# Attention and gated MLP layer on one core: the ordering list in blocks of four matmuls, a GpSimd product, head sums of two slices, three residual buffers, and the spatial weights' load behind the last transpose

## The chip, the cores and the metric

The kernel runs on one core of a Trainium2 chip. A core has a matrix engine (TensorE, PE in the profile, with its weight loads as PEld), a vector engine (VectorE, DVE), a scalar engine for activations and casts (ScalarE, ACT), a general engine (GpSimd, POOL) and an engine that mostly issues DMAs (SyncE, SP). Each works through its own queue in order; semaphores join them. PSUM holds what matmuls accumulate, SBUF all other data on the chip. The metric is the device time of one execution in microseconds (us).

## The reference

2048 rows of 1024 values in bfloat16, one layer of two halves: local attention with 32 heads of 32 values, where each row sees itself and seven earlier rows at steps of two, then a gated MLP whose gate mixes all rows.

```python
def _A_ref(x, wqkv, wo):                  # H = 32, Dh = 32, W, dil = 8, 2
    q, k, v = split(x @ wqkv)
    idx = pos[:, None] - off[None, :]     # off = 0, 2, ..., 14
    logits = einsum('bhsd,bhswd->bhsw', q, k[idx]) * Dh ** -0.5   # masked where idx < 0
    attn = softmax(logits)
    return einsum('bhsw,bhswd->bhsd', attn, v[idx]) @ wo
def _B_ref(x, w_in, w_sp, b_sp, w_out):   # F = 3584, Fh = 1792
    z = gelu(x @ w_in)
    z1 = z[..., :Fh]
    z2 = layernorm(z[..., Fh:])
    g = einsum('ts,bsf->btf', w_sp, z2) + b_sp
    return (z1 * g) @ w_out
h = x + _A_ref(layernorm(x), A_wqkv, A_wo)
h2 = h + _B_ref(layernorm(h), B_w_in, B_w_sp, B_b_sp, B_w_out)
```

## The kernel before

The rows are cut into four chunks of 512 (index `c`), each of four blocks of 128 rows (`il`). Up to line 751 the chunks go through these steps; after it comes a last phase that mixes all rows.

- `ln1(c)`: the first layernorm of the chunk, with a transpose through memory.
- `qkv(c)`: the three projections on PE, 24 groups of 8 matmuls (line 351). Two groups share one accumulator. ScalarE casts it out (lines 358 and 363).
- `attention(c)`: the work of DVE. For each of the eight window places a product of q and the shifted k, 4096 values a partition (line 407), which is then folded by adding halves: 4096 to 2048 values (`add1`, line 411) and, in mode 2, 2048 to 1024 (`add2`, line 414). PE sums the folded slices over the head's lanes with small matmuls (line 430) into `L`. `LMODE` gives each chunk its mode, the number of slices that are left for PE. In mode 2 one sum takes four window places and 8 matmuls of 512 columns, and a chunk has two sums; in mode 4 it takes two places and 16 matmuls of 256 columns, and a chunk has four. Then come the maximum (line 439), the exponential on ScalarE (line 449), the sum and its reciprocal, the broadcast of the weights by PE (line 483) and its copies (line 488), and eight products with the shifted v, added up (lines 501, 504, 510).
- `head(c)`: the output projection on PE, 64 matmuls (line 554), then on DVE the residual sum (line 563) with x from a small buffer `xr` (`XRB` buffers, loaded at line 558), on ScalarE the squares (line 568), the moments in `batch_rstd`, and the normalised rows, transposed by a DMA on SyncE's queue into `hnT` (line 601; line 586 for chunk 3, block by block).
- `b_z2(c)` and `b_z1(c)`: the two halves of the first MLP product on PE (lines 627 and 677), with gelu on ScalarE. z1 goes to memory; z2 is squared (line 643), normalised (lines 656 and 658) and stored.
- `batch_rstd`: four small operations on DVE (lines 519 to 522), a power of -1/2 on GpSimd (line 524), and, where it serves four blocks at once, one small product on DVE again (line 529): minus mean times the root, named nb, which ScalarE's normalisation uses as its bias.
- `wsp0`, line 743: loads the first quarter of the spatial weights by a transposing DMA on SyncE's queue (line 695).
- The last phase, lines 763 to 803: for each chunk 224 matmuls with the spatial weights (line 773), the gate on DVE (lines 776 and 777) and the output projection (line 788).

The order within PE, ScalarE, DVE and GpSimd up to line 751 is not the order of the program. Every step is put on a list with `add(engine, cost in us, function, what it needs, prio, lat, take, free)`, and `Order.run` plays the list through with these costs: it takes the engine on which something can start first, among its steps that can start then (within 0.02 us) the one with the lowest `prio`, and notes its place. `take` and `free` count the three accumulators and other buffers. A need is met `lat` (0.1 us, unless told otherwise) after the needed step's end. The instructions are then written down in that order, and on the chip each engine keeps to it, whatever the real times are. PE's large groups have `prio` 6 and up in the order of the program; head projections have 4 and up, the small sums and broadcasts 1. `LSLACK` and `BSLACK` (2 us) hold a head sum or a broadcast back in the list after its last input. DMAs (`dma_op`) are on the list too, with a place but no engine.

A group of 8 matmuls on PE is one step of 1.727 us in `qkv` and `b_z1`; in `head` and `b_z2` half a block (8 matmuls) is one step. The second step of an accumulator needs the first, 0.1 us after its end.

Of the kernel before, what the change touches and what calls it, by code (L numbers as in the profile page):

```python
# [10 lines left out]
FP32 = mybir.dt.float32  # L11
BF16 = mybir.dt.bfloat16
ALU = mybir.AluOpType
# [7 lines left out]
P = 128  # L21
NT = S // P
CH = 512
NCH = S // CH
# [8 lines left out]
NWARM = 14  # L33
XRB = 2
LMODE = (2, 2, 4, 4)
LSLACK, BSLACK = 2.0, 2.0
Z2ACT = (4, 4, 4, 0)
LNPRIO = (0, 2.0, 2.5, 4.0)
LAST_COLS = ((0, 512), (512, 768), (768, 1024))
# [85 lines left out]
def kernel(  # L125
# [35 lines left out]
    eps_t = cpool.tile([P, 1], FP32, name="eps_t")  # L161
    V.memset(eps_t[:], EPS)
    nhalf = cpool.tile([P, TPC], FP32, name="nhalf")
    V.memset(nhalf[:], -0.5)
# [164 lines left out]
    def qkv(c):  # L329
        for xi in range(3):  # L330
            wv = wsb[xi][:].rearrange("p kt (m dl) -> p kt dl m", dl=DLO)
            for dp in range(DLO // 2):
                key = ("acc", "qkv", c, xi, dp)
                deps = [G.get(("xnT", c))]
                if c == 0 and xi == 0 and dp < 2:
                    def mm(wv=wv, dp=dp):
                        if dp == 0:
                            accs = [new_acc(), new_acc()]
                            G["acc", "qkv", 0, 0, 0], G["acc", "qkv", 0, 0, 1] = accs
                            for kt in range(KT):  # L340
                                for dl in range(4):
                                    T.matmul(accs[dl // 2][:, dl % 2, :], wv[:, kt, dl, :], xnT[0][:, kt, :],  # L342
                                             start=(kt == 0), stop=(kt == KT - 1))
                    last = add("PE", 6.91 if dp == 0 else 0.0, mm, deps, prio=order(), take="acc")
                else:
                    for j in range(2):
                        def mm(j=j, dl=2 * dp + j, wv=wv, key=key):
                            if j == 0:
                                G[key] = new_acc()
                            for kt in range(KT):  # L350
                                T.matmul(G[key][:, j, :], wv[:, kt, dl, :], xnT[c][:, kt, :],  # L351
                                         start=(kt == 0), stop=(kt == KT - 1))
                        last = add("PE", 1.727, mm, deps, prio=order(), take="acc" if j == 0 else None)
                        deps = [last]
                def ev(xi=xi, dp=dp, key=key):
                    if c == 0:
                        off = 0 if xi == 0 else HALO
                        A.copy(att_in[0][xi][:, 2 * dp:2 * dp + 2, off:off + CH], G[key][:])  # L358
                        if xi > 0 and dp == 3:
                            dma(qkv_d[xi][:, :, CH - HALO:CH], att_in[0][xi][:, :, CH:CH + HALO])  # L360
                    else:
                        stg = l1.tile([P, 2, CH], BF16, name="stg", tag="xn", bufs=4)
                        A.copy(stg[:], G[key][:])  # L363
                        dma(qkv_d[xi][:, 2 * dp:2 * dp + 2, c * CH:(c + 1) * CH], stg[:])
# [9 lines left out]
    def attention(c):  # L374
# [67 lines left out]
        prev = add("DVE", 1.18, mx, lms, prio=3.0, take="prod")  # L442
        exps = []
        for hw in range(2):
            ws = slice(4 * hw, 4 * hw + 4)
# [69 lines left out]
    def batch_rstd(key, sums, sqs, n, pfx, deps, prio, cols=TPC):  # L515
        def a1():
            t = {k: bp.tile([P, cols], FP32, name=pfx + k, tag=pfx + k) for k in ("mean", "msq", "var", "rstd", "nb")}
            G[key] = t
            V.tensor_scalar(t["mean"][:], sums(), 1.0 / n, None, op0=ALU.mult)
            V.tensor_tensor(t["msq"][:], t["mean"][:], t["mean"][:], op=ALU.mult)  # L520
            V.scalar_tensor_tensor(t["var"][:], sqs(), 1.0 / n, t["msq"][:], op0=ALU.mult, op1=ALU.subtract)
            V.tensor_scalar(t["var"][:], t["var"][:], 0.0, EPS, op0=ALU.max, op1=ALU.add)
        s1 = add("DVE", 0.74, a1, deps, prio=prio)
        s2 = add("POOL", 1.05, lambda: nc.gpsimd.tensor_tensor(G[key]["rstd"][:], G[key]["var"][:], nhalf[:, 0:cols], op=ALU.pow), [s1], lat=0.4)  # L524
        if cols < TPC:
            return s2
        def a3():
            t = G[key]
            V.scalar_tensor_tensor(t["nb"][:], t["mean"][:], -1.0, t["rstd"][:], op0=ALU.mult, op1=ALU.mult)
        return add("DVE", 0.16, a3, [s2], prio=prio)  # L530

    def head(c):
# [6 lines left out]
        for il in range(TPC):  # L539
            i = c * TPC + il  # L540
            deps = [G["avdone", c]]
            for half in range(2):
                def mm(half=half, il=il, i=i):
                    if half == 0:
                        if il == 0:
# [5 lines left out]
                        st["acc", il] = new_acc()  # L551
                    for dl in range(4 * half, 4 * half + 4):
                        for nh in range(2):
                            T.matmul(st["acc", il][:, nh, :], oTs[c][:, dl, il * P:(il + 1) * P], wo_sb[:, dl, nh * CH:(nh + 1) * CH],  # L554
                                     start=(dl == 0), stop=(dl == DLO - 1))
                def xr_load(k):
                    st["xr", k] = bp.tile([P, D], BF16, name="xr", tag="xr", bufs=XRB)
                    dma(st["xr", k][:], x2d[(c * TPC + k) * P:(c * TPC + k + 1) * P, :])
                m_ = add("PE", 1.727, mm, deps, prio=prio + il * 1e-2 + half * 1e-3, take="acc" if half == 0 else None)
                deps = [m_]  # L560
            def res(il=il, i=i):
# [11 lines left out]
        if last:  # L573
            G["close"] = dma_op(0.0, close_, [G["headmm", c]] + [G["z2n", k, il] for k in range(c) for il in range(TPC)])
            for il in range(TPC):
                rs = batch_rstd(("l2", c, il), lambda il=il: st["hsum"][:, il:il + 1], lambda il=il: st["hsq"][:, il:il + 1],
                                D, f"l2_{il}", [sqd[il]], 0.5, cols=1)
                def nrm(il=il):
                    t = G["l2", c, il]
                    V.tensor_scalar(st["hnc"][:, il, :], st["hnc"][:, il, :], t["mean"][:], t["rstd"][:],  # L580
                                    op0=ALU.subtract, op1=ALU.mult)
                n_ = add("DVE", 0.5, nrm, [rs], prio=0.6)
# [25 lines left out]
    def b_z2(c):  # L608
        st = {}
        sqd = []  # L610
        for il in range(TPC):
            evs = []
            for hf in range(2):
                wd = win_specs[hf][1]
                deps = [G.get(("hnT", c, il), G["hnT", c]), G["win", hf]]
                for half in range(2):
                    def mm(half=half, hf=hf, il=il, wd=wd):
                        if half == 0:
                            st["acc"] = G["accz", c, il, hf] = new_acc()
# [3 lines left out]
                        accf = G["accz", c, il, hf][:].rearrange("p a b -> p (a b)")  # L623
                        for kt in range(4 * half, 4 * half + 4):
                            for n0 in range(0, wd, CH):
                                n1 = min(n0 + CH, wd)
                                T.matmul(accf[:, n0:n1], hnTs[c][:, il, kt, :], wins[hf][:, kt, n0:n1],  # L627
                                         start=(kt == 0), stop=(kt == KT - 1))
                    m_ = add("PE", 1.727 if hf == 0 else 1.3, mm, deps, prio=order(), take="acc" if half == 0 else None)
                    deps = [m_]  # L630
                def ev(hf=hf, il=il, wd=wd):
# [18 lines left out]
        for il in range(TPC):  # L650
            i = c * TPC + il
            def nrm(il=il, i=i):
# [4 lines left out]
                else:  # L657
                    V.tensor_scalar(z2[:], st["u", il][:], t["mean"][:, il:il + 1], t["rstd"][:, il:il + 1], op0=ALU.subtract, op1=ALU.mult)
                if c < NCH - 1:
# [7 lines left out]
    def b_z1(c):  # L667
        for fp in range(NF // 2):
            deps = [G["hnT", c], G["win", 2 if fp < 4 else 3]]
            for j in range(2):  # L670
                def mm(j=j, fp=fp):
                    f = 2 * fp + j
                    wt, f0 = (wins[2], f) if f < 8 else (wins[3], f - 8)
                    if j == 0:
                        G["accy", c, fp] = new_acc()
                    for kt in range(KT):
                        T.matmul(G["accy", c, fp][:, j, :].rearrange("p (a b) -> p a b", a=TPC), wt[:, kt, f0 * P:(f0 + 1) * P],  # L677
                                 hnTs[c][:, :, kt, :], start=(kt == 0), stop=(kt == KT - 1))
# [155 lines left out]
```

## Time and profile before

| what | us |
|---|---|
| time, median of 3 runs | 737.73 (737.09 to 739.45) |
| the profiled execution, its own time | 737.65 |
| its span, first to last instruction | 735.9 |
| head sums, line 430: 32 matmuls of 512 columns, 128 of 256 | busy 2.5 and 5.0 |
| line 414, second fold, 16 of 683 ns | busy 10.4 |
| line 411, first fold, 32 of 1.22 us | busy 38.2 |
| line 407, window products, 32 of 2.28 us | busy 72.0 |
| line 524, power on GpSimd, 7 of four columns | busy 15.7 |
| line 529, small product on DVE, 7 of 0.16 us | busy 1.2, idle before it 5.8 |

The profiled execution is one run under the hardware profiler. Its span stands for what the queues show; 1.75 us of its time lie outside. Rows of the profile name a line, an engine, an operation, the tiles written and read (`acc<-xnT,wv`), the shape and a count; a row's bracket gives the idle time of that engine just before it and what ended it. The granted clock of PE was 0.998 of full speed over the span.

### The profile page before, as it was taken

Reading aid. Unit: us, or ns where it says so; the run is one execution under the profiler, and the core shown is the slowest. Engines: PE = TensorE matmul, PEld = TensorE weight load, DVE = VectorE, ACT = ScalarE, POOL = GpSimd, SP = SyncE. Lnnn points to the kernel's source line nnn. Section 1 sums busy time; section 2 is a strip of 40 time slices with the busy share of each in tenths; the row PEclk is TensorE's granted clock in tenths of the full one; section 3 lists DMA queues with packets and bytes.
Section 4 is the critical chain, followed back from the end, with each engine's and each line's share of the span. In section 5 each row is a group of like instructions: output and inputs, shape, how many; then the busy total and the mean of one; then the engine's idle time right before and its main releaser. Section 6 shows DMA issues by size and latency. Waiting matters only on the chain.

```text
span 735.9 us, 8608 instructions
## 1 busy us (share of the span) xinstructions
PE 725.7 (99%) x3580; PEld 369.1 (50%) x3580; DVE 416.8 (57%) x431; ACT 219.2 (30%) x267; POOL 50.0 (7%) x59
## 2 busy tenths in 40 slices
PE   7999999999999999999999999999999999999998
PEld 4666665566645444444444544444444444444444
DVE  4899899988999899889940012221232223212322
ACT  4322532534338954696563620000000000000000
POOL 0310200100102100300113000000000000000000
PEclk9999999999999999999999999999999999999999
DMA  9874563485484632370079988135104410020002
GB/s 337 315 242 116 191 184 122 153 231 200 149 324 109 210 113 74 115 227 18 29 229 338 256 243 268 40 95 148 58 29 112 133 57 31 28 86 29 1 15 71
DMA packets 113223, 105.27 MB, mean 143 GB/s; under 512 B 67776, under 2 KB 91744, under 8 KB 113056
## 3 DMA queue, kind: packets, MB, share of 16 engines
q1 hardware_dynamic: 105472, 72.63, 33.0%
q0 software_dynamic: 7280, 31.50, 12.1%
q8 instruction: 28, 0.46, 0.3%
q10 hardware_dynamic: 432, 0.59, 0.2%
q14 instruction: 11, 0.09, 0.0%
HBM read 55.09 MB, written 33.88 MB: 121 GB/s over the span
## 4 chain that ended last, share of the span: by engine, by line
PE 89%; DVE 7%; ACT 1%; POOL 1%; issue 1%; DMA 0%; POOLq 0%; DVEq 0%; ACTq 0%
PE acc L773 26%; PE acc L351 22%; PE acc L788 13%; PE acc L627 10%; PE acc L677 9%; PE acc L554 8%; DVE prod L504 2%; DVE oT L510 2%; PE acc L342 1%; DVE part L411 1%; POOL l3rstd L524 1%; PE L L430 1%; DMA xp<-in_A_x_dram 0%; PE tpa L252 0%; ACT z1s L683 0%
## 5 line engine op out<-in xcount | busy, mean ns | idle before, releaser
L773 PE MATMUL acc<-wspT,z2sb 128*128 128x512 bf16 x896 | 194.0, 379 | 0.0
L773 PEld LDWEIGHTS <-z2sb 128*128 128x128 bf16 x896 | 87.7, 98 | 105.7
L776 DVE TENSOR_TENSOR g<-acc,bB 128x1024 bf16<-128x1024 f32 x28 | 34.3, 1224 | 157.6 <-PE acc L773 133.0
L677 PE MATMUL acc<-hnT,win 128*128 128x512 bf16 x448 | 99.4, 379 | 0.5 <-ACT z1s L683 0.5
L627 PE MATMUL acc<-win,hnT 128*128 128x512 bf16 (+1 forms) x512 | 99.3, 352 | 0.0
L627 PEld LDWEIGHTS <-hnT 128*128 128x128 bf16 x512 | 49.8, 98 | 47.7 <-issue 0.9
L407 DVE TENSOR_TENSOR prod<-qT,kT 128x4096 bf16<-128x4096 bf16 x32 | 72.0, 2284 | 1.6 <-ACT kT L358 1.6
L788 PEld LDWEIGHTS <-zg 128*128 128x128 bf16 x462 | 45.2, 98 | 51.7
L677 PEld LDWEIGHTS <-win 128*128 128x128 bf16 x448 | 43.4, 98 | 52.5 <-issue 1.7
L504 DVE TENSOR_TENSOR prod<-vT,AB 128x4096 bf16<-128x4096 bf16 x28 | 63.8, 2289 | 1.0
L510 DVE TENSOR_TENSOR oT<-oT,prod 128x4096 bf16<-128x4096 bf16 x28 | 64.0, 2284 | 0.1
L363 ACT CAST stg<-acc 128x1024 bf16<-128x1024 f32 x36 | 36.4, 1011 | 78.6 <-PE acc L351 75.5
L788 PE MATMUL acc<-wout_a,zg 128*128 128x512 bf16 (+1 forms) x264 | 58.2, 373 | 0.0
L795 DVE TENSOR_TENSOR ot<-acc,hr 128x1024 bf16<-128x1024 f32 x15 | 18.4, 1224 | 69.4 <-PE acc L788 69.4
L351 PE MATMUL acc<-xnT,wv 128*128 128x512 bf16 x256 | 57.1, 380 | 0.0
L351 PE MATMUL acc<-xnT,wk 128*128 128x512 bf16 x256 | 57.1, 380 | 0.0
L554 PE MATMUL acc<-wo_sb,oT 128*128 128x512 bf16 x256 | 56.3, 379 | 0.7 <-DVE oT L510 0.7
L351 PE MATMUL acc<-xnT,wq 128*128 128x512 bf16 x224 | 49.8, 379 | 0.0
L351 PEld LDWEIGHTS <-wk 128*128 128x128 bf16 x256 | 36.4, 143 | 19.1 <-issue 0.9
L351 PEld LDWEIGHTS <-wv 128*128 128x128 bf16 x256 | 36.4, 143 | 19.1 <-issue 0.9
L788 PE MATMUL acc<-wout_b,zg 128*128 128x512 bf16 (+1 forms) x198 | 44.4, 373 | 0.0
L351 PEld LDWEIGHTS <-wq 128*128 128x128 bf16 x224 | 31.9, 143 | 16.8 <-issue 0.8
(125 smaller groups left out, 489.9 us busy)
## 6 DMA issues: line engine op xcount, KB each, us to landing
qkv_d<-stg SPq DMA_DIRECT2D x36, 256.0 KB, 2.5
z_d<-z1s SPq DMA_DIRECT2D x28, 256.0 KB, 2.6
z1c<-z_d SPq DMA_DIRECT2D x28, 256.0 KB, 2.7
z_d<-u SPq DMA_DIRECT2D x12, 448.0 KB, 2.9
z2sb<-z_d POOLq DMA_DIRECT2D x12, 448.0 KB, 9.2
xr<-in_A_x_dram SPq DMA_DIRECT2D x16, 256.0 KB, 2.8
h_d<-hb SPq DMA_DIRECT2D x16, 256.0 KB, 2.4
win<-in_B_w_in_dram POOLq DMA_DIRECT2D x2, 2048.0 KB, 9.1
```

Of the source, the lines that this page charges most:

```text
L351: T.matmul(G[key][:, j, :], wv[:, kt, dl, :], xnT[c][:, kt, :], start=(kt == 0), stop=(kt == KT - 1))
L363: A.copy(stg[:], G[key][:])
L407: V.tensor_tensor(st["prod"][:], qT[:], kT[:, :, o:o + CH], op=ALU.mult)
L504: V.tensor_tensor(pvs[w][:], vT[:, :, o:o + CH], abb, op=ALU.mult)
L510: prev = add("DVE", 2.3, lambda w=w: V.tensor_tensor(oTs[c][:], oTs[c][:], pvs[w][:], op=ALU.add), [prev, m_], prio=3.0, lat=0.15, free="p ...
L554: T.matmul(st["acc", il][:, nh, :], oTs[c][:, dl, il * P:(il + 1) * P], wo_sb[:, dl, nh * CH:(nh + 1) * CH], start=(dl == 0), stop=(dl == ...
L627: T.matmul(accf[:, n0:n1], hnTs[c][:, il, kt, :], wins[hf][:, kt, n0:n1], start=(kt == 0), stop=(kt == KT - 1))
L677: T.matmul(G["accy", c, fp][:, j, :].rearrange("p (a b) -> p a b", a=TPC), wt[:, kt, f0 * P:(f0 + 1) * P], hnTs[c][:, :, kt, :], start=(kt ...
L773: T.matmul(acc[:, j, :], z2sb[a][:, f * P:(f + 1) * P], wspT[:, a, :], start=(a == 0), stop=(a == NT - 1))
L776: V.tensor_tensor(g1[:], acc[:], bB[:, c * CH:(c + 1) * CH].unsqueeze(1).to_broadcast([P, 2, CH]), op=ALU.add)
L788: T.matmul(outs, zg[:, f, il * P:(il + 1) * P], wt[:, f0, lo:hi], start=(f == 0), stop=(f == NF - 1))
L795: V.tensor_tensor(ot[:], acc[:].rearrange("p a b -> p (a b)"), hr[:], op=ALU.add)
```

## The change

The edits:

1. `LMODE` is 2 for all four chunks.
2. PE's groups go on the list in blocks of four matmuls: in `qkv` and `b_z1` a group of eight is two steps of 0.863 us (`PIECES`), in `head` a block of rows has four steps instead of two, in `b_z2` too (0.863 or 0.653 us). The next block of an accumulator may follow at once (0.0 in place of the 0.1 us).
3. In `batch_rstd` the product nb moves from DVE to GpSimd, right behind the power; the list counts both as one step of 1.6 us whose result is there 1.2 us later. For this the mean is kept with a minus sign, and what subtracted it adds it.
4. In chunks 0 and 1 an exponential of one value per partition stands on ScalarE ahead of the real ones, as soon as the head sums are done.
5. `XRB` is 3: three residual blocks are loaded at the start of a head, and the fourth after the first block's squares.
6. `wsp0` needs chunk 3's last transpose too.
7. Names: `moments` and `root` for what was `a1`, the power and `a3`.

```diff
-XRB = 2
-LMODE = (2, 2, 4, 4)
+XRB = 3
+LMODE = (2, 2, 2, 2)
+PIECES = ((0, 0), (0, 4), (1, 0), (1, 4))
...
+    texp = cpool.tile([P, 1], FP32, name="texp")
...
-                    for j in range(2):
-                        def mm(j=j, dl=2 * dp + j, wv=wv, key=key):
-                            if j == 0:
+                    for j, k0 in PIECES:
+                        def mm(j=j, k0=k0, dl=2 * dp + j, wv=wv, key=key):
+                            if j == 0 and k0 == 0:
                                 G[key] = new_acc()
-                            for kt in range(KT):
+                            for kt in range(k0, k0 + 4):
                                 T.matmul(G[key][:, j, :], wv[:, kt, dl, :], xnT[c][:, kt, :],
                                          start=(kt == 0), stop=(kt == KT - 1))
-                        last = add("PE", 1.727, mm, deps, prio=order(), take="acc" if j == 0 else None)
-                        deps = [last]
+                        last = add("PE", 0.863, mm, deps, prio=order(), take="acc" if j == 0 and k0 == 0 else None)
+                        deps = [(last, 0.0)]
...
+        if c < 2:
+            add("ACT", 0.2, lambda: A.activation(texp[:], eps_t[:], ACTF.Exp), lms, prio=0.0, table="exp")
...
-            V.tensor_scalar(t["mean"][:], sums(), 1.0 / n, None, op0=ALU.mult)
-            V.tensor_tensor(t["msq"][:], t["mean"][:], t["mean"][:], op=ALU.mult)
+            V.tensor_scalar(t["nmean"][:], sums(), -1.0 / n, None, op0=ALU.mult)
+            V.tensor_tensor(t["msq"][:], t["nmean"][:], t["nmean"][:], op=ALU.mult)
...
-        s2 = add("POOL", 1.05, lambda: nc.gpsimd.tensor_tensor(G[key]["rstd"][:], G[key]["var"][:], nhalf[:, 0:cols], op=ALU.pow), [s1], lat=0.4)
-        if cols < TPC:
-            return s2
-        def a3():
-            t = G[key]
-            V.scalar_tensor_tensor(t["nb"][:], t["mean"][:], -1.0, t["rstd"][:], op0=ALU.mult, op1=ALU.mult)
-        return add("DVE", 0.16, a3, [s2], prio=prio)
+        def root():
+            t = G[key]
+            nc.gpsimd.tensor_tensor(t["rstd"][:], t["var"][:], nhalf[:, 0:cols], op=ALU.pow)
+            if cols == TPC:
+                nc.gpsimd.tensor_tensor(t["nb"][:], t["nmean"][:], t["rstd"][:], op=ALU.mult)
+        return add("POOL", 1.05 if cols < TPC else 1.6, root, [s1], lat=0.4 if cols < TPC else 1.2)
...
-            for half in range(2):
+            for part in range(4):
...
-                    for dl in range(4 * half, 4 * half + 4):
+                    for dl in range(2 * part, 2 * part + 2):
...
-                m_ = add("PE", 1.727, mm, deps, prio=prio + il * 1e-2 + half * 1e-3, take="acc" if half == 0 else None)
-                deps = [m_]
+                m_ = add("PE", 0.863, mm, deps, prio=prio + il * 1e-2 + part * 1e-3, take="acc" if part == 0 else None)
+                deps = [(m_, 0.0)]
...
-                        for kt in range(4 * half, 4 * half + 4):
+                        for kt in range(2 * part, 2 * part + 2):
...
-                    m_ = add("PE", 1.727 if hf == 0 else 1.3, mm, deps, prio=order(), take="acc" if half == 0 else None)
-                    deps = [m_]
+                    m_ = add("PE", 0.863 if hf == 0 else 0.653, mm, deps, prio=order(), take="acc" if part == 0 else None)
+                    deps = [(m_, 0.0)]
...
-            for j in range(2):
-                def mm(j=j, fp=fp):
+            for j, k0 in PIECES:
+                def mm(j=j, k0=k0, fp=fp):
...
-                m_ = add("PE", 1.727, mm, deps, prio=order(), take="acc" if j == 0 else None)
-                deps = [m_]
+                m_ = add("PE", 0.863, mm, deps, prio=order(), take="acc" if j == 0 and k0 == 0 else None)
+                deps = [(m_, 0.0)]
...
-    dma_op(0.0, wsp0, [G["z1ev", NCH - 2], G["close"]])
+    dma_op(0.0, wsp0, [G["z1ev", NCH - 2], G["close"], G["hnT", NCH - 1]])
```

The normalisations at lines 580 and 658 use `nmean` with an addition in place of `mean` with a subtraction.

More of the change, by code (lines that the diff above doesn't have):

```diff
@@ L515, in batch_rstd, with moments @@
     def batch_rstd(key, sums, sqs, n, pfx, deps, prio, cols=TPC):
-        def a1():
-            t = {k: bp.tile([P, cols], FP32, name=pfx + k, tag=pfx + k) for k in ("mean", "msq", "var", "rstd", "nb")}
+        def moments():
+            t = {k: bp.tile([P, cols], FP32, name=pfx + k, tag=pfx + k) for k in ("nmean", "msq", "var", "rstd", "nb")}
             G[key] = t
-            V.tensor_scalar(t["mean"][:], sums(), 1.0 / n, None, op0=ALU.mult)
-            V.tensor_tensor(t["msq"][:], t["mean"][:], t["mean"][:], op=ALU.mult)
+            V.tensor_scalar(t["nmean"][:], sums(), -1.0 / n, None, op0=ALU.mult)
+            V.tensor_tensor(t["msq"][:], t["nmean"][:], t["nmean"][:], op=ALU.mult)
             V.scalar_tensor_tensor(t["var"][:], sqs(), 1.0 / n, t["msq"][:], op0=ALU.mult, op1=ALU.subtract)
             V.tensor_scalar(t["var"][:], t["var"][:], 0.0, EPS, op0=ALU.max, op1=ALU.add)
-        s1 = add("DVE", 0.74, a1, deps, prio=prio)
-        s2 = add("POOL", 1.05, lambda: nc.gpsimd.tensor_tensor(G[key]["rstd"][:], G[key]["var"][:], nhalf[:, 0:cols], op=ALU.pow), [s1], lat=0.4)
-        if cols < TPC:
-            return s2
-        def a3():
+        s1 = add("DVE", 0.74, moments, deps, prio=prio)
+        def root():
             t = G[key]
-            V.scalar_tensor_tensor(t["nb"][:], t["mean"][:], -1.0, t["rstd"][:], op0=ALU.mult, op1=ALU.mult)
-        return add("DVE", 0.16, a3, [s2], prio=prio)
+            nc.gpsimd.tensor_tensor(t["rstd"][:], t["var"][:], nhalf[:, 0:cols], op=ALU.pow)
+            if cols == TPC:
+                nc.gpsimd.tensor_tensor(t["nb"][:], t["nmean"][:], t["rstd"][:], op=ALU.mult)
+        return add("POOL", 1.05 if cols < TPC else 1.6, root, [s1], lat=0.4 if cols < TPC else 1.2)
     def head(c):
@@ L541, in head, with mm @@
             deps = [G["avdone", c]]
-            for half in range(2):
-                def mm(half=half, il=il, i=i):
-                    if half == 0:
+            for part in range(4):
+                def mm(part=part, il=il, i=i):
+                    if part == 0:
                         if il == 0:
@@ L579, in nrm @@
                     t = G["l2", c, il]
-                    V.tensor_scalar(st["hnc"][:, il, :], st["hnc"][:, il, :], t["mean"][:], t["rstd"][:],
-                                    op0=ALU.subtract, op1=ALU.mult)
+                    V.tensor_scalar(st["hnc"][:, il, :], st["hnc"][:, il, :], t["nmean"][:], t["rstd"][:],
+                                    op0=ALU.add, op1=ALU.mult)
                 n_ = add("DVE", 0.5, nrm, [rs], prio=0.6)
@@ L615, in b_z2, with mm @@
                 deps = [G.get(("hnT", c, il), G["hnT", c]), G["win", hf]]
-                for half in range(2):
-                    def mm(half=half, hf=hf, il=il, wd=wd):
-                        if half == 0:
+                for part in range(4):
+                    def mm(part=part, hf=hf, il=il, wd=wd):
+                        if part == 0:
                             st["acc"] = G["accz", c, il, hf] = new_acc()
@@ L657, in nrm @@
                 else:
-                    V.tensor_scalar(z2[:], st["u", il][:], t["mean"][:, il:il + 1], t["rstd"][:, il:il + 1], op0=ALU.subtract, op1=ALU.mult)
+                    V.tensor_scalar(z2[:], st["u", il][:], t["nmean"][:, il:il + 1], t["rstd"][:, il:il + 1], op0=ALU.add, op1=ALU.mult)
                 if c < NCH - 1:
@@ L669, in b_z1 @@
             deps = [G["hnT", c], G["win", 2 if fp < 4 else 3]]
-            for j in range(2):
-                def mm(j=j, fp=fp):
+            for j, k0 in PIECES:
+                def mm(j=j, k0=k0, fp=fp):
                     f = 2 * fp + j
                     wt, f0 = (wins[2], f) if f < 8 else (wins[3], f - 8)
-                    if j == 0:
+                    if j == 0 and k0 == 0:
                         G["accy", c, fp] = new_acc()
-                    for kt in range(KT):
+                    for kt in range(k0, k0 + 4):
                         T.matmul(G["accy", c, fp][:, j, :].rearrange("p (a b) -> p a b", a=TPC), wt[:, kt, f0 * P:(f0 + 1) * P],
                                  hnTs[c][:, :, kt, :], start=(kt == 0), stop=(kt == KT - 1))
-                m_ = add("PE", 1.727, mm, deps, prio=order(), take="acc" if j == 0 else None)
-                deps = [m_]
+                m_ = add("PE", 0.863, mm, deps, prio=order(), take="acc" if j == 0 and k0 == 0 else None)
+                deps = [(m_, 0.0)]
             def ev(fp=fp):
```

## The prediction

> **What bounds the kernel now.** I read the page first: the busy shares, then the chain that ended last. TensorE (PE) holds 89% of that chain and is busy for 99% of the span; the vector engine (DVE) holds 7%, nearly all of it between 300 and 368 us.
>
> ```profile
> PE 725.7 (99%) x3580; PEld 369.1 (50%) x3580; DVE 416.8 (57%) x431; ACT 219.2 (30%) x267; POOL 50.0 (7%) x59
> ...
> PE 89%; DVE 7%; ACT 1%; POOL 1%; issue 1%; DMA 0%; POOLq 0%; DVEq 0%; ACTq 0%
> ```
>
> The 57% of DVE is a mean over two stages. By the timeline of DVE alone, from 42.23 us to 368.07 us it runs the four chunks' attention with hardly a pause, and PE fills in projections around it. After 368 us PE runs without any wait to the end. So the question is what PE loses before 368 us; the timeline of PE has it:
>
> ```profile
> 249.60 1.89 PE L677 MATMUL acc<-hnT,win 128*128 128x512 bf16 x8 [0.45 <-ACT z1s L683]
> ...
> 320.86 0.62 PE L430 MATMUL L<-part,csb 128*32 128x256 bf16 x16 [1.31 <-DVE part L411]
> ...
> 356.87 10.52 PE L677 MATMUL acc<-hnT,win 128*128 128x512 bf16 x48
> 368.13 13.99 PE L554 MATMUL acc<-wo_sb,oT 128*128 128x512 bf16 x64 [0.74 <-DVE oT L510]
> 381.95 10.52 PE L677 MATMUL acc<-hnT,win 128*128 128x512 bf16 x48
> 392.31 1.89 PE L627 MATMUL acc<-win,hnT 128*128 128x512 bf16 x8
> 394.04 1.89 PE L677 MATMUL acc<-hnT,win 128*128 128x512 bf16 x8
> ```
>
> Start, length, what, and in brackets the idle time before it. Three waits, 0.45 + 1.31 + 0.74 = 2.50 us in all. And a cushion: when the last head begins at 368.13, PE still has 48 + 8 = 56 matmuls of chunk 2's z1 in hand, which need nothing of chunk 3. At 1.727 us for 8 (the pitch 392.31 to 394.04) that is 12.1 us.
>
> **PE work that goes.** The chain shows a head sum of either kind at the same price:
>
> ```profile
> 74.65 0.55 PE L L430 x8
> ...
> 217.68 0.55 PE L L430 x16
> ```
>
> Chunks 2 and 3 do four sums each of 16 matmuls now and two each of 8 afterwards: 8 - 4 = 4 fewer, 4 x 0.55 = 2.2 us. The block of eight behind one takes 1.83 instead of 1.73 us, so up to 2.6; I take **-2.4 us**. Blocks of four instead of eight issue the same matmuls: 0. With every wait of the three gone too, the floor is 735.9 - 2.4 - 2.5 = 731.0 us.
>
> **What DVE gets in exchange.** Each of the 16 window products of chunks 2 and 3 gains the second fold of line 414. Its price stands in chunk 0:
>
> ```profile
> 46.64 2.35 DVE L411 TENSOR_TENSOR prod<-prod 128x2048 bf16<-128x2048 bf16 x2
> 48.91 1.28 DVE L414 TENSOR_TENSOR part<-prod 128x1024 bf16<-128x1024 bf16 x2
> 50.11 4.49 DVE L407 TENSOR_TENSOR prod<-qT,kT 128x4096 bf16<-128x4096 bf16 x2
> ...
> 307.51 0.16 DVE L529 SCALAR_TENSOR_TENSOR l2nb<-l2mean,l2rstd 128x4 f32<-128x4 f32 x1 [0.93 <-POOL l2rstd L524]
> ```
>
> Two folds from 48.91 to 50.11: 0.60 each, 16 x 0.60 = **+9.6 us**, all in the stage where DVE has no pause.
>
> The last line is what comes back. The small product nb leaves DVE, which now stands still for the root that GpSimd (POOL) computes. There are six such places before 368 us with waits of 0.93, 0.92, 0, 0.93, 0.90 and 0.90, sum 4.58, and 0.08 of pitch each, 0.5: at best -5.1 us. But why does that root take so long?
>
> ```profile
> 242.39 1.02 POOL L524 TENSOR_TENSOR l3rstd<-l3var,nhalf 128x4 f32<-128x4 f32 x1 [2.35 <-DVE l3var L522]
> ...
> 304.57 2.90 POOL L524 TENSOR_TENSOR l2rstd<-l2var,nhalf 128x4 f32<-128x4 f32 x1 [23.39 <-DVE l2var L522]
> ```
>
> 1.02 us beside a product that reads PSUM, 2.90 us beside a 4096-wide product with both inputs in SBUF (304.30 to 306.58); it ended 0.89 us after that product did. Now DVE won't pause behind it, and a second POOL operation follows. If DVE must stand aside for both, it pays 2 x 0.9 in each of six places, 10.8, instead of 5.1: +5.7 at worst. No row shows which; I take half of the best, **-2.5**, since the root's wait is the only thing proved and a small operation need not hold DVE for all of its 0.9 us.
>
> The Trainium skill has a rule on this (SBUF — State Buffer, "Who interferes with whom"): a DVE instruction with two SBUF inputs and a GpSimd instruction that reads SBUF exclude each other for a whole instruction, and whichever issues first blocks the other fully. The 2.90 us root agrees with it. Read strictly it speaks against this change, since each POOL operation would then hold the next product; the sum by the rule would be the +5.7, the one without it the -5.1.
>
> DVE also waits for PE: 3.2 for head sums (maximum, line 439), 5.4 for the broadcast (line 488), 2.45 of line 563's 9.2 before 368 us. These sit behind blocks of eight, 1.727 us; with blocks of four the mean wait for the block in progress falls by 0.43. For eight such events (four maxima, four casts) 3.5 us at best, 0 at worst; I take **-2.0**, as part of these waits is the chain's own latency.
>
> The shift of chunk 3's last attention product is therefore s = 9.6 - 2.5 - 2.0 = **+5.1 us**, with ends 9.6 - 5.1 - 3.5 = +1.0 and 9.6 + 5.7 = +15.3.
>
> **From DVE's shift to PE's end.** PE's work ahead of the last head ends at 367.39 now (368.13 - 0.74), and at 367.39 - 2.4 - 0.45 - 1.31 = 363.23 with less to do and no waits. The last product ends at 368.07 + s. The gap is covered with z1 matmuls if the planner puts them there; I assume that it does, since the fold is in its list at 0.60. But not all 12.1 us are free: after the head, PE needs something until the first transpose of chunk 3 lands, 378.58 (issue, first line below) + 6.7 (median of that transfer) = 385.3, 3.2 us after the head ends at 382.1. So 8.9 us are free and s may reach 363.23 + 8.9 - 368.07 = 4.06 for nothing; what is above is PE idle, one for one. With s = 5.1 that is 1.0. New waits behind finer pieces I price at 0.5, between 0 and the 1.31 that the largest costs now. Span: 731.0 + 1.0 + 0.5 = 732.5.
>
> **Edits that I cost at nothing.** The third residual buffer: the same 16 loads, and DVE's waits at line 563 all name PE, not the load; if a load came late, it would delay one residual sum by 2.8, its median landing. The early exponential: chunk 0's table load (1.28 us at 75.76) already ends before its input is ready, and chunk 1 has none; what waits behind it on ScalarE is a cast, and the one there now stood idle for 4.21 us before it began (74.73). The spatial weights' load:
>
> ```profile
> 378.58 2.79 SPq L586 DMA_TRANSPOSE hnT<-hb  x2
> ...
> 387.45 3.97 SPq L586 DMA_TRANSPOSE hnT<-hb  x1
> 391.52 10.11 SPq L684 DMA_DIRECT2D z_d<-z1s  x3
> 401.73 11.95 SPq L695 DMA_TRANSPOSE wspT<-in_B_w_sp_dram  x1
> ```
>
> It already stands behind the last transpose on SyncE's queue. At worst it moves in front of the three z1 stores, which would then wait up to 11.95 us; their four buffers are next wanted at 422.8, so nothing waits. It landed at 415.7, and PE wants it at 442.4: 26 us of cover. The sign change of the mean is the same instruction. Groups that no longer interleave cost nothing and even out ScalarE's evictions.
>
> **Time.** The profiled execution took 737.65 us, 1.75 around its span of 735.9, and the median is 737.73. I add 1.8: **734.3 us**, 0.5% below. Within 0.3% (2.2 us) of the median counts as no change here: 735.5 to 739.9.
>
> **Rivals.**
> *The fold eats the gain.* If nothing of the POOL waits or of the waits for PE comes back, s = 9.6: idle 9.6 - 4.06 = 5.5, span 731.0 + 5.5 + 0.5 = 737.0, **738.8 us**. For it: DVE has no pause in chunks 2 and 3, and 9.6 is the surest term here. Against: the 4.58 us of waits are real, and the instruction that waits is taken out.
> *POOL and the products get in each other's way.* Place: the six roots. Price: s = 15.3, idle 11.2, span 731.0 + 11.2 + 0.5 = 742.7, **744.5 us**, slower. It decides from s = 9.0 on (731.0 + 4.94 = 735.9). A worse form of it: the pair finds no gap until DVE pauses, at 320.8 instead of 307.5 for chunk 2; ScalarE, in order, holds its evictions behind the normalisation, and PE runs out of accumulators after two groups, 6.9 us, so 6.4 is lost each time. For it: the root made no headway at all beside the product. Against: DVE's queue shows a small gap between products already.
> *The list does not do what it says* (no z1 is moved in front of the head): PE idles 368.07 + 5.1 - 363.23 = 9.9, span 741.4, **743.2 us**; it goes with the second rival. Against it: the order is computed anew from the same costs, and now misses DVE's real end by only 0.74.
>
> **How the numbers follow.** Forecast 0.58, first rival 0.24, second with the third 0.18. The forecast's own range is 732.6 (s at most 4.06, no new wait, 2.6 for the sums) to 735.5. The whole range goes down to 731.5 for bounds that may be loose and up to 741.0, s = 11.5 or so, which leaves out the second rival's upper part. Faster 0.58, same 0.24, slower 0.18.
>
> **What would show it.** Right: line 430 with 64 matmuls, all of 512 columns; DVE's fold 32 times; no wait of DVE on a root before the last head; the last head's start some 5 us later with fewer z1 matmuls behind it. Wrong: products longer than 2.29 us or idle time naming POOL; POOL operations of 4 us and more; PE waits before the last head or the first line 627 of chunk 3 over 2 us; ScalarE standing at line 596.

## The result and the profile after

| | before | changed |
|---|---|---|
| time, median of 5 runs each, us | 737.8 | 733.97 |
| ratio, with its 95% interval | | 0.9936 (0.9915 to 0.9957) |
| profiled execution: time, span, us | 737.65, 735.9 | 733.6, 731.8 |
| PE waits between the start and the last phase, us | 2.50 | 0.91 |
| chunk 3's last attention product ends, us | 368.07 | 370.62 |
| z1 matmuls left behind the last head | 56 | 20 |

The kernel became 0.6% faster: 3.8 us by the medians, 4.1 by the spans. Here and in the experiments the ratio leaves out runs more than 1.5% above a kernel's fastest, as two of the changed kernel's five are (751.37 and 767.65 us, without a trace and with an open cause), while medians and ranges keep them.

First the timeline of PE after, in the columns of the one before.

```profile
241.24 0.61 PE L432 MATMUL L<-part,csb 128*32 128x512 bf16 x8 [0.68 <-DVE part L416]
...
351.96 20.02 PE L680 MATMUL acc<-hnT,win 128*128 128x512 bf16 x92
371.82 13.98 PE L557 MATMUL acc<-wo_sb,oT 128*128 128x512 bf16 x64
385.63 4.48 PE L680 MATMUL acc<-hnT,win 128*128 128x512 bf16 x20
389.95 24.38 PE L630 MATMUL acc<-win,hnT 128*128 128x512 bf16 x128
414.16 24.34 PE L680 MATMUL acc<-hnT,win 128*128 128x512 bf16 x112
438.34 6.85 PE L776 MATMUL acc<-wspT,z2sb 128*128 128x512 bf16 x31
```

No wait stands at the last head, though attention ends 2.55 us later: 92 of chunk 2's 112 z1 matmuls are now in front of it, and 20 behind. The last phase begins at 438.34 instead of 442.43. One wait of 0.68 for a head sum and one of 0.23 for a broadcast are what is left of 2.50.

Next the places where GpSimd works beside DVE's products, around the root of chunk 0, DVE's timeline first.

```profile
139.49 1.22 DVE L413 TENSOR_TENSOR prod<-prod 128x2048 bf16<-128x2048 bf16 x1
140.63 2.28 DVE L409 TENSOR_TENSOR prod<-qT,kT 128x4096 bf16<-128x4096 bf16 x1
142.83 0.68 DVE L416 TENSOR_TENSOR part<-prod 128x1024 bf16<-128x1024 bf16 x1
```

```profile
139.67 1.94 POOL L530 TENSOR_TENSOR l2rstd<-l2var,nhalf 128x4 f32<-128x4 f32 x1 [23.39 <-DVE l2var L526]
141.68 1.28 POOL L532 TENSOR_TENSOR l2nb<-l2nmean,l2rstd 128x4 f32<-128x4 f32 x1
```

GpSimd stretches (its product takes 1.28 us here, and 0.20 us at 243.31, beside a product that reads PSUM). DVE does not: its rows follow each other without idle time and last as long as before.

Last, SyncE's queue behind the last head.

```profile
388.75 3.27 SPq L589 DMA_TRANSPOSE hnT<-hb  x2
392.12 0.71 SPq L687 DMA_DIRECT2D z_d<-z1s  x1
392.93 25.58 SPq L698 DMA_TRANSPOSE wspT<-in_B_w_sp_dram  x1
418.87 7.27 SPq L687 DMA_DIRECT2D z_d<-z1s  x3
```

As before, the weights' transpose follows the last transposes of chunk 3 and what is left of chunk 2's z1 stores, but that is one store now instead of three. It is issued at 392.9 instead of 401.7 and holds the queue for 25.6 us instead of 12.0. Its data land 40.4 us after the issue, at 433.3, 5 us before PE wants them. ScalarE waited 7.5 us for a z1 store behind it; PE did not.

### The profile page after: what moved, and what is told of

The parts are those of the page before. It is cut to its first block, busy times and chain, and to the rows that moved or that the text cites. A ratio compares the mean times of both kernels' runs of the same rounds, so it can differ in the third digit from the quotient of the medians.

```text
span 731.8 us, 8429 instructions
## 1 busy us (share of the span) xinstructions
PE 723.2 (99%) x3484; PEld 367.2 (50%) x3484; DVE 426.4 (58%) x440; ACT 220.9 (30%) x269; POOL 51.7 (7%) x66
## 3 DMA queue, kind: packets, MB, share of 16 engines
q0 software_dynamic: 7280, 31.50, 12.8%
## 4 chain that ended last, share of the span: by engine, by line
PE 84%; DVE 6%; issue 5%; DMA 5%; ACT 0%; POOL 0%; DVEq 0%; POOLq 0%
PE acc L776 26%; PE acc L353 13%; PE acc L791 13%; PE acc L680 13%; PE acc L630 11%; PE acc L557 6%; DMA xp<-in_A_x_dram 3%; DVE prod L409 2%; DMA xr<-in_A_x_dram 1%; DVE prod L413 1%; DVE bnst L226 1%; DVE bnst L227 1%; DMA xn_d<-xn 1%; DVE part L416 1%; DVE xn L246 0%
```

## The experiments

Twelve kernels, each timed beside the kernel before. All ratios are against that kernel.

| run | what | median, us | lowest to highest | ratio (95%) |
|---|---|---|---|---|
| undo_fold | changed, old `LMODE` | 737.04 | 734.35 to 766.5 | 0.9973 (0.996 to 0.9986) |
| undo_nb | changed, nb on DVE | 757.26 | 742.46 to 765.63 | 1.012 (1.0078 to 1.0163) |
| undo_blocks | changed, steps of eight | 743.9 | 734.47 to 775.98 | 0.9987 (0.9965 to 1.001) |
| blocks8_no_gap | the same, without the 0.1 us | 757.78 | 754.49 to 760.25 | 1.026 (1.0235 to 1.0285) |
| fold_alone | before, new `LMODE` | 757.11 | 756.14 to 775.97 | 1.0263 (1.025 to 1.0276) |
| nb_alone | before, nb on GpSimd | 735.8 | 735.39 to 737.62 | 0.9971 (0.9959 to 0.9984) |
| six_more_pool | changed, six more GpSimd products a root | 734.77 | 733.11 to 773.7 | 0.9941 (0.9919 to 0.9963) |
| fold_twice_c3 | changed, chunk 3's fold twice | 758.95 | 750.49 to 761.37 | 1.0266 (1.0227 to 1.0305) |
| late_weights | changed, weights behind the z2 loads | 749.05 | 744.75 to 753.46 | 1.0144 (1.0115 to 1.0173) |
| fold_alone_late | fold_alone with that | 743.82 | 742.7 to 749.79 | 1.0077 (1.006 to 1.0095) |
| fold_twice_late | fold_twice_c3 with that | 749.92 | 748.7 to 753.42 | 1.0168 (1.0145 to 1.0191) |
| undo_nb_late | undo_nb with that | 738.37 | 735.85 to 744.51 | 1.0009 (0.9991 to 1.0027) |

### The parts taken back, one at a time

**undo_fold**

```diff
-LMODE = (2, 2, 2, 2)
+LMODE = (2, 2, 4, 4)
```

> The changed kernel with LMODE (2, 2, 4, 4) again; all else as changed. Theory (PE sets the time, and what DVE needs more is hidden behind z1 matmuls that PE still has in hand): four more head sums at 0.55 us and what stands behind them, 2.4 us of PE more, DVE 9.6 us less to do, which gives nothing: span 731.8 + 2.4 = 734.2, time 736.0. Rival (the fold is a loss that the other edits pay for): 9.6 us less on DVE brings the time below 733, span 731 or less.

0.9973 against 0.9936: the fold is worth 0.0037 x 737.8 = 2.7 us where all else is changed, with some 1.8 us either way by the two intervals. The traces say 2.3: the span is 735.6, 3.8 more, but the first window product also begins 1.5 us later (44.04 against 42.53). That is the price of the head sums (2.4 expected): DVE's 9.6 us less gave PE nothing that shows, since DVE did not set the end. The last head's z1 in hand went from 20 matmuls to 68.

**six_more_pool**

```diff
                 nc.gpsimd.tensor_tensor(t["nb"][:], t["nmean"][:], t["rstd"][:], op=ALU.mult)
+                for _ in range(6):
+                    nc.gpsimd.tensor_tensor(t["msq"][:], t["nmean"][:], t["rstd"][:], op=ALU.mult)
```

> The changed kernel with six more GpSimd products of 4 columns behind each nb of four columns, written to a scratch tile that nobody reads; the list does not know of them. Theory (a GpSimd operation slips in when a DVE product ends and costs DVE nothing): DVE's products keep their 2.28 and 1.22 us and their pitch, chunk 3's last product ends at 370.6 within 0.5, time 734.0 within 0.3%. Rival (each of them holds DVE for 0.2 to 0.9 us): 36 of them before the last head, 7 to 32 us on DVE, of which 3.9 are covered: time 737 to 762.

The timelines of GpSimd and DVE in this run, at chunk 1's root:

```profile
220.85 1.29 POOL L532 TENSOR_TENSOR l2nb<-l2nmean,l2rstd 128x4 f32<-128x4 f32 x1
222.09 7.92 POOL L534 TENSOR_TENSOR l2msq<-l2nmean,l2rstd 128x4 f32<-128x4 f32 x6
```

```profile
219.79 4.49 DVE L409 TENSOR_TENSOR prod<-qT,kT 128x4096 bf16<-128x4096 bf16 x2
224.20 2.35 DVE L413 TENSOR_TENSOR prod<-prod 128x2048 bf16<-128x2048 bf16 x2
226.47 1.28 DVE L416 TENSOR_TENSOR part<-prod 128x1024 bf16<-128x1024 bf16 x2
```

Six products take 7.92 us of GpSimd, 1.32 each, and the DVE rows beside them start one after the other and last as in every other place. Chunk 3's last product ends at 370.14 (370.62 without the extra work), but DVE's first window product begins 1.03 us earlier in this run (41.50). From first to last DVE takes 0.55 us more, and one wait for an exponential of ScalarE has grown from 1.45 to 2.59. ScalarE came late there because it had waited 3.22 us for nb, whose root stood on GpSimd's queue behind six of the extra products. So the rival's 7 to 32 us are not there: GpSimd waits, DVE's rows do not. What 36 extra operations cost, they cost through the results that came late behind them.

**nb_alone**

```diff
-        return add("DVE", 0.16, a3, [s2], prio=prio)
+        return add("POOL", 1.05 if cols < TPC else 1.6, root, [s1], lat=0.4 if cols < TPC else 1.2)
```

> The kernel before with nb on GpSimd behind the root and the list's cost of it (1.6, 1.2), and nothing else. Theory: DVE's six waits of 0.9 us and the small product go, 5.1 us of DVE; the two PE waits that name DVE (1.31 and 0.74) go, nothing else does: span 733.9 to 734.5, time 735.7 to 736.3. Rival (GpSimd holds the products): products of 2.28 us and their folds stretch or stand behind GpSimd, time as before, 737.7, or longer.

735.8, inside the 735.7 to 736.3 expected; span 733.7. In its trace both PE waits on DVE (1.31 and 0.74) are gone, the 0.45 for an accumulator too, and one of 0.42 for a residual sum is new. So the GpSimd product alone, with the order that the list makes of it, brings 0.29% (0.16 to 0.41).

**undo_blocks** and **blocks8_no_gap** (the second keeps `deps = [(last, 0.0)]`)

```diff
-PIECES = ((0, 0), (0, 4), (1, 0), (1, 4))
+PIECES = ((0, 0), (1, 0))
...
-                        last = add("PE", 0.863, mm, deps, prio=order(), take="acc" if j == 0 and k0 == 0 else None)
-                        deps = [(last, 0.0)]
+                        last = add("PE", 1.727, mm, deps, prio=order(), take="acc" if j == 0 and k0 == 0 else None)
+                        deps = [last]
```

> The changed kernel with the list's steps of eight matmuls again (1.727 us, 0.1 us between the steps of one accumulator). Theory: DVE's waits for head sums and broadcasts (4.9 us before the last head now, 8.6 before the change) come back, 2 to 3.5 us, nearly all covered; a wait of 0.45 us for an accumulator can come back: span 732 to 733, time 734 to 735. Rival (the blocks are the gain): PE waits of 2.5 us and more, time 736.5 or above.

> The changed kernel with steps of eight matmuls, but with 0.0 instead of 0.1 us between the steps of one accumulator. It parts the size of the steps from the order of the groups. Theory: the gain of the blocks, if any, lies in DVE's waits for a sum behind a step (size), so this is like undo_blocks within 1 us of span. Rival (it is the groups that no longer interleave): like the changed kernel, span 731.8, and undo_blocks is slower.

The first came out in part. Its profiled run (span 732.8) is what I expected, but its twelve runs spread over 40 us, and by the ratios it is 0.5% slower than the changed kernel. The reason I gave is not in the trace: DVE waits 1.7 + 4.0 = 5.7 us for head sums and broadcasts, against 4.9 with blocks of four, and the last product ends at 369.3, 1.3 us earlier than the changed kernel's (1.0 of it is an earlier start). What PE loses there comes after the head:

```profile
407.82 6.23 PE L630 MATMUL acc<-win,hnT 128*128 128x512 bf16 x32 [2.77 <-DMA hnT<-hb]
```

It waits for chunk 3's last transposed block, which was issued beside the z2 loads and landed 18.1 us after its issue (12.8 in the changed kernel, where PE does not wait).

The second came out 22 us above either expectation, so it cannot part size from order. Its PE waits 22.3 us in one piece, for a transposed block of chunk 3, which is the subject of the next part.

### What stands behind the runs of 757 us

**fold_alone**

```diff
-LMODE = (2, 2, 4, 4)
+LMODE = (2, 2, 2, 2)
```

> The kernel before with LMODE (2, 2, 2, 2) and nothing else. Theory, by the prediction's formula: s = 9.6, PE idle 9.6 - 4.06 = 5.5 in place of the three waits, span 731.0 + 5.5 = 736.5 to 737.0, time 738.3 to 738.8. Rival (no cover at all): 735.9 - 2.4 + 9.6 = 743.1, time 744.9. Rival (the fold alone brings the gain): span 733.5 or less, time 735.3.

None of the three. PE's idle time is not where DVE is late; it comes after the head. PE's timeline and SyncE's queue:

```profile
423.93 14.91 PE L627 MATMUL acc<-win,hnT 128*128 128x512 bf16 x63 [17.71 <-DMA hnT<-hb]
```

```profile
389.48 4.39 SPq L586 DMA_TRANSPOSE hnT<-hb  x2
393.97 0.53 SPq L565 DMA_DIRECT2D h_d<-hb  x1
394.60 25.44 SPq L695 DMA_TRANSPOSE wspT<-in_B_w_sp_dram  x1
420.14 0.53 SPq L565 DMA_DIRECT2D h_d<-hb  x1
420.76 3.76 SPq L586 DMA_TRANSPOSE hnT<-hb  x2
```

The weights' transpose stands between the second and the third transpose of chunk 3 and holds the queue for 25.4 us. The span without the 20.1 us of waits for hnT would be 736.2, near the prediction's 737.0 for this case; the prediction did not have the 20.

**undo_nb** (the list's costs go back too)

```diff
-            if cols == TPC:
-                nc.gpsimd.tensor_tensor(t["nb"][:], t["nmean"][:], t["rstd"][:], op=ALU.mult)
+        def a3():
+            t = G[key]
+            V.scalar_tensor_tensor(t["nb"][:], t["nmean"][:], 1.0, t["rstd"][:], op0=ALU.mult, op1=ALU.mult)
+        return add("DVE", 0.16, a3, [s2], prio=prio)
```

> The changed kernel with nb computed by DVE again and the list's costs for the root as before (1.05, 0.4). Theory: DVE stands still again at the roots, five or six times 0.9 us, so chunk 3's last product ends some 5 us later, at 375 to 376 instead of 370.6. Of that about 3.9 us are covered (the head starts 1.2 us after the product now; 20 z1 matmuls of 4.3 us are left behind the head, of which the transposes need 1.6): PE idle of 1 to 2 us more, span 733 to 734, time 735 to 736. Rival (the cover takes it all): 734.0 and no PE wait at the head. Rival (nothing is covered): span 736.8, time 738.6.

Missed too. DVE's last product ends at 371.2, not at 375: in the new order DVE waits three times 0.9 us for a root before the last head, and less for PE. The traced run, 757.27, has no PE wait at the head, but 5.9 us for hnT and 14.4 for a z1 eviction, while the weights' transpose holds SyncE for 50.6 us. The ratio rests on two runs alone (742.46 and 750.34), of which there is no trace; what these lost, and where, isn't shown.

**fold_twice_c3**

```diff
                 if mode == 2:
+                    if c == 3:
+                        pr_ = add("DVE", 0.60, add2, [pr_], prio=3.0)
                     pr_ = add("DVE", 0.60, add2, [pr_], prio=3.0, free="prod")
```

> The changed kernel with the second fold of chunk 3 done twice (the same result is written again), 0.60 us each in the list as well: DVE needs 8 x 0.60 = 4.8 us more before the last head. Theory: 3.9 us of it are covered by z1 matmuls that move in front of the head, about 1 us shows as PE idle, before the head or before chunk 3's first z2 group: span 732.8, time 734.6 to 735.0. Rival (no cover is left): span 736.6, time 738.4. Rival (the cover is larger): time 734.0, no PE wait.

Again the weights stand ahead of the last two transposes (390.4, for 18.0 us), and PE waits 25.5 us for hnT. Ahead of that its trace says what was asked; the run below repeats it.

**late_weights, fold_alone_late, fold_twice_late, undo_nb_late** (one edit, on four kernels; `last_store` is as before, and in fold_alone_late `wsp0` needs the last transpose too)

```diff
     def wsp0():
+        probe = dma(probe_d[:, :], z2sb[(NCH - 1) * TPC - 1][:, 0:8])
         i_ = load_wsp(0)
+        tc.add_manual_dep(i_.ins, probe.ins.name, ...)
```

> The changed kernel with one small store of 8 values per partition of the last loaded z2 block to a scratch, put on SyncE's queue ahead of the first spatial weights' transpose, so that this transpose waits until the twelve z2 loads have landed. Theory (the transpose, issued at 392.9 us beside the z2 loads, holds SyncE's queue for 25 us and more, and the runs of 751 and 768 us are those in which this grew): the transpose's issue takes 12 us or less as in the kernel before, its load lands before 428 us, time 734.0 within 0.3%, and every run within 1% of the lowest. Rival (those runs have another cause): the time is the same, and some runs still exceed 745.

> fold_alone with the same small store ahead of the weights' transpose, which also stands behind the last transpose of chunk 3. Theory (19.1 us of fold_alone's PE waits for hnT came from the weights' transpose standing ahead of the last two transposes on SyncE's queue; without it the prediction's first rival holds): PE waits for DVE and for transposes of 3 to 6 us in all, span 736 to 737, time 738 to 739. Rival (the fold itself costs the 20 us): time 757 again. Rival (the fold alone brings the gain): 735.3 or less.

> fold_twice_c3 with the same small store. Theory: the cover is used up but hardly exceeded (in fold_twice_c3 the last head began at 375.99 without a wait, with no z1 left behind it): PE idle of 0 to 1.5 us more than the changed kernel, span 732 to 733.5, time 734 to 735.3. Rival (no cover): 738.4.

> undo_nb with the same small store. Theory (what undo_nb lost beyond 735 to 736 was again the weights' transpose, whose issue held SyncE's queue for 50 us): PE waits of 14.4 and 5.9 us go, time 735 to 736, all runs within 1%. Rival (nb on DVE costs this by itself): 742 and above. Rival (nb's place doesn't matter to PE at all): 734.0.

My theory of the slow transpose fell in its narrow form: late_weights should have stayed at 734 and took 745 to 753 in every run. Its SyncE queue:

```profile
415.32 0.33 SPq L748 DMA_DIRECT2D probe_d<-z2sb  x1
415.70 31.66 SPq L699 DMA_TRANSPOSE wspT<-in_B_w_sp_dram  x1
447.45 1.58 SPq L688 DMA_DIRECT2D z_d<-z1s  x3
```

Behind the last z2 load the transpose takes 31.7 us, longer than beside them: the output weights' loads of GpSimd's queue (2048 KB at 414.76, 1536 KB at 421.31) are there now. The z1 stores behind it come at 447, ScalarE has no buffer, and PE waits 10.0 us for an accumulator. Such a wait costs more than its length: in the 3.8 us behind it PE's granted clock is 0.50. So the z2 loads aren't special. Issue times of the first weights' transpose, with GpSimd's large loads beside it:

| kernel | issued at, us | takes, us | large loads issued |
|---|---|---|---|
| before | 401.7 | 12.0 | z2 until 395.6, the next at 416.1 |
| nb_alone | 399.6 | 11.6 | z2 until 393.3, the next at 413.9 |
| undo_fold | 395.5 | 17.2 | z2 until 395.9, the next at 415.8 |
| undo_blocks | 391.7 | 21.8 | z2 until 398.4, the next at 413.0 |
| changed | 392.9 | 25.6 | z2 until 401.7, the next at 412.0 |
| late_weights | 415.7 | 31.7 | output weights at 414.8 and 421.3 |
| fold_twice_c3 | 390.4 | 18.0 | z2 from 393.6 until 410.4 |
| undo_nb | 391.2 | 50.6 | z2 from 389.3 until 404.4, output weights at 418.5 and 425.1 |
| before, its shortest | | 7.3 | |

The other six traced kernels take 19.5 to 30.5. The quick place, 12 us, is the gap between the issues of the two sets of loads; beside either set it is 17 us and more. How far into the loads it starts does not order the times: fold_twice_c3 starts ahead of them all and takes 18.0. Whether that is the DMA engines' share or the queues' order isn't settled.

Of the four, two fulfil a part. fold_alone_late gives back 13.7 of fold_alone's 19.4 us (0.0186 and 0.0263 of 737.8): the wait of 17.71 us is gone, but the last two transposes now start together with the z2 loads (397.87 and 397.32) and PE still waits 11.1 us for them in the traced run, at 749.79 us the slowest of seven. undo_nb_late stands at 738.4, a ratio of 1.0009 against undo_nb's 1.012, 2 us above what was expected. A wait for hnT is left:

```profile
411.69 7.84 PE L632 MATMUL acc<-win,hnT 128*128 128x512 bf16 x31 [3.92 <-DMA hnT<-hb]
```

The last transposed block was issued at 391.19, beside the z2 loads, and landed 20.5 us later, long before the weights' transpose was issued (414.91). So chunk 3's own transposes are slowed by these loads too; in the kernel before, the last one took 19.0 us to land and PE had other work until then. And fold_twice_late answers the question of the cover, on PE's timeline:

```profile
351.66 24.34 PE L683 MATMUL acc<-hnT,win 128*128 128x512 bf16 x112
375.83 13.98 PE L560 MATMUL acc<-wo_sb,oT 128*128 128x512 bf16 x62
389.64 10.54 PE L633 MATMUL acc<-win,hnT 128*128 128x512 bf16 x52
```

All 112 z1 matmuls are in front of the head, which starts without a wait, and chunk 3's z2 follows it without a wait (two of the head's 64 records are missing from this trace). DVE's 4.8 us more cost PE nothing up to there. The time of 749.9 comes after: PE waits 13.3 us behind the late weights, as in late_weights.

No run here beats the changed kernel. Holding the output weights' loads back until the spatial weights are through was not tried.

## Why the prediction was right, point by point

It said 734.3, and the time is 733.97; the span was to be 732.5 and is 731.8. What bounds the kernel and why the fold is hidden was right. That the number is so near is in part luck: some terms were right by size, some cancelled, and one failed without a cost in the traced run.

- **Head sums, -2.4:** right. 64 matmuls of 512 columns stand where 160 stood; taking the fold back costs 2.7.
- **PE's waits, from 2.50 to 1.5 (1.0 of idle and 0.5 of new ones):** 0.91. With 0.31 us of a later start of the first projection in this run, the span is -2.7 - 1.6 + 0.3 = -4.0, measured -4.1.
- **The fold's +9.6 on DVE:** right, and hidden, as said. The last product ended 2.55 us later, not 5.1; s was inside its ends of 1.0 and 15.3. Its terms don't simply add: 9.6 - 5.1 - 3.7 (the roots, and the waits for PE's sums and broadcasts) would be 0.8; new waits of 1.17 us for a residual block and 1.01 for a store (78.83) are part of the rest.
- **nb's price:** half of the gain was too little. No wait on a root is left before the last head, so all of the 5.1 us came back. That GpSimd might hold DVE, the ground for the half, is refuted by six_more_pool, where DVE's rows keep their length. The rule of the Trainium skill (SBUF — State Buffer, "Who interferes with whom") holds here on one side only: GpSimd waits for the product that runs (1.28 against 0.20 us), while no DVE row here waits for GpSimd.
- **The blocks' -2.0 on DVE's waits:** not shown. The sums' and broadcasts' waits fell from 8.6 to 4.9, more than that, but with blocks of eight they are 5.7. It is the new order as a whole; the size of the steps and the 0.1 us together account for 0.8. The ratios (0.9987 with eight, 0.9936 with four) say that the blocks are worth something all the same; in the one trace of it that is the wait of 2.77 us for a transposed block, a place that the prediction did not look at.
- **The cover, 8.9 of 12.1 us:** right that z1 moves ahead of the head, too small in size. The 3.2 us that were to bridge to the first transpose aren't needed: in fold_twice_late the last product ends at 375.34, s = 7.3, no z1 is left and PE goes straight on. So s may reach some 7 us, and the "1.0 of idle" was nothing. It holds only while the last transposes land in time: undo_blocks and undo_nb_late, with 16 and 12 z1 matmuls left, wait 2.8 and 3.9 us for the last one.
- **The third residual buffer at nothing:** DVE waited 1.17 us for a residual block in chunk 1 (217.53), so the load is late there; it is hidden. nb_alone, with two buffers, has such a wait of 1.2 as well.
- **The spatial weights at nothing, with 26 us of cover:** this step failed, though its zero came out. I took the landing at 415.7 from before and asked only whether the three z1 stores would suffer. But those stores were what kept the transpose waiting until the z2 loads were through. With fewer z1 groups behind the head, it starts 9 us earlier, beside the loads, and lands 18 us later: 5 us of cover instead of 26. That nothing of this reached PE is luck; in fold_alone, fold_twice_c3 and blocks8_no_gap it did. The edit that is to put it behind the last transpose does not bind either: SyncE's order isn't made by the list, blocks8_no_gap and fold_twice_c3 have the edit and yet the transpose ahead, and in the changed kernel the order on every queue is the same without it.

**The rivals.** The first (the fold eats the gain, 738.8) was tested by fold_alone and came out at 757.1, by a mechanism that I hadn't listed; without most of it, 743.8. The second fell with six_more_pool, the third with the 92 z1 matmuls in front of the head. Whether the changed kernel would gain from a weights' transpose that collides with nothing stays open: late_weights, built to decide it, moved the collision instead of removing it.

## What to carry to other kernels

When one engine sets the time and another is nearly full, count the work in hand that can move in front of the late result; within it, work shifted onto the second engine was free here (that beyond it the cost is one for one is the prediction's assumption, which no run tests). When that work moves, look at what it used to delay: a transfer that was harmless because a store held it back may start early and collide. And an order that is written for four engines says nothing of the fifth queue; look where its long DMA really stands.

## What the runs showed of the hardware

- Small GpSimd operations beside DVE's back-to-back products of two SBUF inputs took 1.1 to 1.6 us each instead of 0.2 to 0.3, and DVE's rows kept their length and order: 30 of the 36 extra ones of six_more_pool stood so. A result that waits behind them on GpSimd's queue comes late.
- A transposing load of 2 MB held its queue for 7.3 to 7.7 us at its shortest, and the first of each run for 17 to 32 us (50.6 once) beside ordinary loads from another queue; what stood behind it on the queue waited as long. In fold_alone PE stood 17.7 us in one wait behind it.
- Smaller transposes are hit too: chunk 3's last one landed 12 to 24 us after its issue where z2 loads stood beside it, against 3.6 to 3.9 for the first two in the kernel before.
- After a wait of 22.3 us (blocks8_no_gap) PE's granted clock was 0.50 for the next 3.4 us.
